# Attention tails issued one row half at a time in units 7 to 15, with a wider margin for planned idling

## The chip, the cores and the metric

The kernel is written in Bass for one Trainium2 chip and runs as one program on one of its cores. The metric is the device time of one execution in microseconds (us). A core has five engines with a queue each: TensorE (PE in the profile; its weight loads are shown as PEld), VectorE (DVE), ScalarE (ACT), GpSimd (POOL) and SyncE (SP, which here only issues DMAs). Every queue is worked off in order, and engines wait for each other by semaphores.

## The reference

Cosine-similarity attention over 8 batches, 12 heads, 448 positions and 64 dimensions, followed by a two-layer feed-forward network with the activation h cos(h) over the 3584 tokens of 768 features:

```python
q_n = q / (norm(q) + 1e-6);  k_n = k / (norm(k) + 1e-6)
attn = softmax(q_n @ k_n.T / tau)              # tau = 0.1
x = (attn @ v).transpose(0, 2, 1, 3).reshape(3584, 768)
h = x @ w_in                                   # 768 -> 2048
out = (h * cos(h)) @ w_out                     # 2048 -> 768
```

## The kernel before

**Units and groups.** A unit is half a batch, six heads; there are 16. A unit has three groups of two heads, so there are 48 groups, numbered g, with unit u = g // 3. The two heads of a group are stacked: head a lies on partitions 64a to 64a+63 of the transposed operands.

**One group's attention.** 448 key positions are three blocks of 128 and a rest of 64. `scores(g, c)` (lines 716 to 736) makes the scores of block c (c = 0 is the rest, c = 1 to 3 the full blocks) with four 64x64 products: head a uses array rows 64a to 64a+63. The rest is arranged so that all 128 rows of the result are used: the upper and the lower 64 partitions hold the rest's scores for two different halves of the queries (o = 0 and 1; the queries are seven strips of 64, each of two halves of 32 columns). ACT then takes the exponential into `PX` (full blocks) or `PH` (the rest).

`attend(g, ...)` (line 739 on) multiplies by the values and makes the sums of the exponentials. Its stages are 0 and 1 (the tails, that is the rest) and 2 (the full blocks):

- Stages 0 and 1 are `rest(e, n)`, line 761: four 64x64 products of 224 columns each. Step n multiplies the values with the half o = n, on rows 64n to 64n+63, and at the same time sums the other half on the other 64 rows, against ones. Step 1 is marked as `settled` on step 0: it waits until step 0 has ended. The scripts below write `a` for stage 0, `b` for stage 1 and `c` for stage 2.
- Stage 2 is `av` (line 768), the values against the three full blocks in four column groups of 32, and, for a group that isn't "direct", the sums: `sm` (line 776, blocks 1 and 2 side by side, 448 columns) and `sm2` (line 784, block 3, two halves of 224 columns in the four column groups).

Groups in `direct` (0 to 5, 7 to 11, 17, 23 and 47) get their reciprocals on ACT by logarithm and exponential. For the others `chain(u)` (line 885) gathers the sums of a unit with DMAs into 128 partitions (`gather`, two DMAs, line 889), adds the parts and takes the reciprocal on VectorE (lines 901 and 904), writes it to DRAM (`spread`, line 905) and reads it back broadcast (`bcast`, line 907); POOL multiplies (line 911) and so makes `xT`, the input of the first layer.

**The network.** `m1` is the first layer of one batch (96 products of 128x128 by 448 columns, line 919), with a cosine on ACT (line 948) and a product on VectorE (line 950) for each two feature blocks. The second layer works on tiles of 128 tokens: `m2_quarters` (line 1017) makes a tile with four 64x64 products at a time, 16 fours in a first half and 16 in a second, where the two row halves exchange their PSUM banks. The first four of the second half is `settled` on the last of the first. When a tile is done, VectorE copies it out of PSUM.

**Order of the work.** TensorE's order from group 19 on is written by hand in `PLAN["script"]`: `s33.0` is a score block, `f5` five fours of the second layer as filling, `m4` a first layer. All else is ordered by a planner: `arrange` computes due times from costs, and `play` runs through the work, where an engine takes the most urgent operation that is ready. It idles for one that is not yet ready if that one is due earlier by more than `PLAN["margin"]` (1.0 us) and comes within `hold` (0.6 us) or half the ready one's cost. The time before the first data is filled with warm-up products on zeros (`zt`, lines 1075 and 1076).

Of the kernel before, what the change touches and what calls it, by code (L numbers as in the profile page):

```python
# [6 lines left out]
ACT = mybir.ActivationFunctionType  # L7
ALU = mybir.AluOpType
# [10 lines left out]
    "swapped": {},  # L19
    "script": {19: """  # L20
# [8 lines left out]
        s32.1 f2 a31 f2 b31 s32.2 f5 s32.3 f7 a32 s33.0 f5 s33.1 f5 s33.2 f6 b32 c32 s33.3 f10 m4 f6  # L29
        a33 s34.0 f8 s34.1 f8 b33 c33 s34.2 f5 s34.3 f5 s35.0 f6 s35.1 f5 s35.2 f4 s35.3 f4 a34 f3 b34 s36.0 c34 c35  # L30
        s36.1 a35 f3 b35 f1 s36.2 f6 s36.3 f6 a36 s37.0 f5 s37.1 f5 s37.2 f6 b36 c36
        s37.3 f4 s38.0 f4 s38.1 f4 s38.2 f4 s38.3 f4 a37 f2 b37 s39.0 c37 c38 s39.1 a38 f3 b38 f1 s39.2 f3 s39.3 f3 m5 c39
        a39 f4 s40.0 b39 f4 s40.1 f4 s40.2 f2 s40.3 f2 s41.0 s41.1 f4 s41.2 f5 s41.3 f5 a40 f2 b40 s42.0 c40 c41
        s42.1 a41 f3 b41 f1 s42.2 f4 s42.3 f4 s43.0 f4 s43.1 f4 s43.2 f5 s43.3 f5 a42 f2 b42 s44.0 c42 c43
        s44.1 f2 a43 f2 b43 s44.2 f5 s44.3 f7 a44 s45.0 f5 s45.1 f5 s45.2 f6 b44 c44 s45.3 f10 o012 m6 f6 s46.0 a45 f12 s46.1 b45 f4 c45 s46.2 f3 s46.3 f4
# [9 lines left out]
    "margin": 1.0,  # L45
# [370 lines left out]
def bass_cosine_attention__then__act_gcu_kernel(  # L416
# [13 lines left out]
    UP = 3  # L430
# [13 lines left out]
    NT = 3  # L444
    TD, LT = PLAN["turned"], 9
# [27 lines left out]
    lnn = sbs("lnn", 2, [128, UH * NB], F32)  # L473
# [4 lines left out]
    PX = sbs("PX", 2, [128, NB * S], BF16)  # L478
    xu = sb("xu", [128, 5 * UP * S], F32)
    RB = sbs("RB", 2, [128, UP * S], F32)  # L480
    sums = sbs("sums", 2, [128, 2 * SPR], F32)
    rcp = sbs("rcp", 2, [128, SPR], F32)
# [3 lines left out]
    zt = sb("zt", [128, S], BF16)  # L486
    ones = sb("ones", [128, 128], BF16)
    iot = cosb[0].bitcast(I32).ap()[:, 0:128]
# [17 lines left out]
    PXv = [t.ap()[:, 0 : NT3 * 2 * S].rearrange("p (c a s) -> p c a s", c=NT3, a=2) for t in PX]  # L506
    PHv = [t.ap()[:, NT3 * 2 * S : NB * S].rearrange("p (a s) -> p a s", a=2) for t in PX]
    xuv = xu.ap().rearrange("p (r g s) -> p r g s", r=5, g=UP)
# [15 lines left out]
    HALF = 0.096  # L524

# [49 lines left out]
    pool(lambda e: e.memset(ones.ap().rearrange("p (x y) -> p x y", y=32)[:, 0:4:3], 0.0), (), ["zeros"], 0.12)  # L575
    sel = [gT.bitcast(F32).ap()[:, (f * RING + S) // 2 : (f * RING + S) // 2 + 128] for f in (NF - 2, NF - 1)]
# [65 lines left out]
    lnnv = [t.ap().rearrange("p (h s) -> p h s", h=UH) for t in lnn]  # L642
    rnv = [t.ap().rearrange("p (h s) -> p h s", h=UH) for t in rn]

    def rnorm(u, p0, p1, t=(0, 1)):
# [5 lines left out]
        if u in PLAN["roots"] or (u, p0) in PLAN["roots"]:  # L651
# [6 lines left out]
        act(lambda e: e.activation(lnnv[i][:, h, w], n2v[i][:, h, w], ACT.Ln, bias=cst.ap()[:, 1:2]),  # L658
            [("n2", i, p, z) for p, z in keys] + ["cst1"], [("lnn", i, p, z) for p, z in keys],
            n, "E", 1, "ln" + tag)  # L660
        act(lambda e: e.activation(rnv[i][:, h, w], lnnv[i][:, h, w], ACT.Exp, scale=-0.5),  # L661
            [("lnn", i, p, z) for p, z in keys], [("rn", i, p, z) for p, z in keys], n, "E", 0, "rn" + tag)
# [47 lines left out]
    def scores(g, c, bank=None):  # L710
# [5 lines left out]
        def full(e):  # L716
            for o in range(2):
                for a in range(2):
                    r = slice(64 * a, 64 * a + 64)
                    m = e.matmul(ph[BP * o : BP * o + BP, a, 0:S], t[r, c - 1 + (NT3 + 1) * o, 0:BP],  # L720
                                 t[r, :, BP : 2 * BP], start=True, stop=True)
            return m

        def half(e):
            for o in range(2):
                for a in range(2):
# [8 lines left out]
        act(lambda e: e.activation(PHv[j] if c == 0 else PXv[j][:, c - 1], ph[:, :, 0:n], ACT.Exp, scale=1.0 / TAU),  # L735
            keys, [("PX", j, c)], 2 * n, "E", label="exp%d.%d" % (g, c))

    opened, held, turned = {}, {}, set(PLAN["swapped"])

    def attend(g, direct, stages=(0, 1, 2)):  # L740
# [8 lines left out]
        folded, swapped = g in PLAN["folded"], g in turned  # L749

        def rest(e, n):
            for k in range(2):
                o = n ^ k
                r = slice(BP * o, BP * o + BP)
                for a in range(2):
                    w = vav[y][r, 2 * p + a, 0 if o else VS - 1, :] if k == 0 else ones.ap()[r, ws]
                    to = AVq[64 * a : 64 * a + 64, k, :, o, :]
                    if folded and k:
                        w = ones.ap()[r, 64 - 64 * o : 128 - 64 * o]
                        to = av_[64 * a : 64 * a + 64, 1, 0 : S // 2]  # L760
                    m = e.matmul(to, w, PHv[j][r, a, :],  # L761
                                 start=(n == 0 and g not in PLAN["quarters"] and not swapped), stop=(n == 1 and swapped))
            return m
# [8 lines left out]
        def sm(e):  # L772
            for n in range(2):
                for a in range(2):
                    o = 64 * a + 32 * n
                    t = e.matmul(av_[o : o + 32, 1, 0:S], ones.ap()[:, 32:64], PXv[j][:, n, a, :],
                                 start=swapped, stop=False)
            return t

        def sm2(e):  # L780
            for n in range(2):
                for a in range(2):
                    o, w = 64 * a + 32 * n, slice(S // 2 * n, S // 2 * n + S // 2)
                    t = e.matmul(av_[o : o + 32, 1, w], ones.ap()[:, 32:64], PXv[j][:, 2, a, w],  # L784
                                 start=False, stop=not swapped)
            return t
# [32 lines left out]
        for n in stages:  # L819
            if n < 2:  # L820
                o = P.op("PE", lambda e, n=n: rest(e, n), [("va", y), ("PX", j, 0), "ones", "zeros"], both_keys,
# [17 lines left out]
        if not direct:  # L839
            if 2 in stages:  # L840
                P.op("PE", sm, ["ones", ("PX", j, 1), ("PX", j, 2)], [ks], cost=MM, mode="C32", label="S%d" % g)
                P.op("PE", sm2, ["ones", ("PX", j, 3)], [ks], cost=HALF, mode="C32", label="S%d" % g)
# [3 lines left out]
            both = bass.AP(xu, (u % 3 * UP + p) * S, [[5 * UP * S, 128], [(3 + i - u % 3) * UP * S, 2], [1, S]])  # L846
# [9 lines left out]
        if folded:  # L856
            s, r = xuv[:, 3 + i, p, 0 : S // 2], RBv[i][:, p, 0 : S // 2]
# [14 lines left out]
        act(lambda e: e.activation(xuv[:, 3 + i, p, :], av_[:, 1, 0:S], ACT.Ln), [ks], [("xs", i, p)], S, "E",  # L872
            label="lnS%d" % g, bias=PLAN["bs"] if g < PB else 0.0)
        act(lambda e: e.activation(r, xuv[:, 3 + i, p, :], ACT.Exp, scale=-1.0), [("xs", i, p)], [("RB", i, p)], S, "E",  # L874
# [10 lines left out]
    def chain(u):  # L885
        i, b = u % 2, u // 2
        n = sum(UP * u + p not in PLAN["direct"] for p in range(UP))
        w = SPR // UP * n
        dma("SP", [lambda e, r=r: e.dma_start(
            sums[i].ap()[:, w * r : w * r + w],  # L890
# [462 lines left out]
```

## Time and profile before

| what | value |
|---|---|
| median of 3 runs | 421.1 us (420.59 to 423.0) |
| the profiled execution | 420.54 us, span 418.8 us |
| granted TensorE clock, mean | 0.999 |
| busy share PE, ACT, POOL, DVE | 98, 65, 58, 45% |
| second layer, fours of 64x64 (L1017) | 2816 products |
| first layer (L919) | 768 products |
| tails (L761) | 384 products |

In the profile L761 is line 761 of the kernel before. A group of instructions is shown as result <- operands, the shape of an instruction and how often it occurs (x8). Lines in the order of time begin with the start and the length in us; the end of a matrix product is modelled, and products overlap, so a slot is read from one start to the next.

### The profile page before, as it was taken

What the parts mean: (1) busy time and instruction counts of PE and PEld (TensorE: products, weight loads), DVE (VectorE), ACT (ScalarE), POOL (GpSimd) and SP (SyncE); (2) the same over time, 40 slices, a digit from 0 to 9 for tenths busy, and PEclk for the clock granted to TensorE, in tenths of its full rate; (3) what the DMA queues carried; (4) which work ended last, traced back from release to release, by engine and by line L of the source; (5) the groups of instructions that cost most, each with busy time, mean ns of one, the idle gap of its engine ahead of it and who ended that gap; (6) DMA issues with size and microseconds to landing.
All of it is one profiled execution on the core that took longest, in us unless ns stands there. A gap on an engine that the chain in (4) does not pass through costs nothing.

```text
span 418.8 us, 13571 instructions
## 1 busy us (share of the span) xinstructions
PE 409.6 (98%) x6074; PEld 236.5 (56%) x6074; DVE 189.5 (45%) x250; ACT 271.3 (65%) x363; POOL 242.7 (58%) x193
## 2 busy tenths in 40 slices
PE   7899999999999999999999999999999999999997
PEld 3354556655556555665466555665566655565565
DVE  3564744456663277124753087213862244223421
ACT  5887578983987746877498556776498745703500
POOL 4999977989761666938864782907867320020000
PEclk9999999999999999999999999999999999999999
DMA  8999999879849997579766993949966720141023
GB/s 191 251 253 226 209 223 172 213 174 198 144 104 151 207 222 185 109 168 217 168 114 127 210 242 83 147 109 212 212 123 128 161 68 3 41 121 38 2 67 85
DMA packets 80254, 63.61 MB, mean 152 GB/s; under 512 B 44996, under 2 KB 75204, under 8 KB 80196
## 3 DMA queue, kind: packets, MB, share of 16 engines
q1 hardware_dynamic: 61988, 50.06, 55.4%
q0 software_dynamic: 18048, 12.59, 20.2%
q8 instruction: 48, 0.79, 0.8%
q10 hardware_dynamic: 160, 0.10, 0.1%
q14 instruction: 10, 0.08, 0.1%
HBM read 54.98 MB, written 11.13 MB: 158 GB/s over the span
## 4 chain that ended last, share of the span: by engine, by line
PE 92%; ACT 4%; POOL 1%; DVE 1%; DMA 1%; issue 1%; SPq 0%; ACTq 0%; POOLq 0%
PE MP L1017 27%; PE SC L919 21%; PE AV L919 11%; PE SC L720 6%; PE AV L768 4%; PE MP L1046 4%; PE SC L1046 3%; PE SC L768 2%; PE AV L761 2%; PE AV L794 2%; PE MP L919 2%; ACT PX L735 2%; PE SC L728 1%; ACT cosb L948 1%; PE MP L809 1%; PE AV L1046 1%
## 5 line engine op out<-in xcount | busy, mean ns | idle before, releaser
L735 ACT ACTIVATE PX<-SC 128x896 bf16<-128x896 f32 (+1 forms) x166 | 132.8, 828 | 26.1 <-PE SC L720 18.2
L1017 PE MATMUL MP<-W,gT 64*64 64x384 bf16 x2816 | 142.3, 324 | 0.9 <-DVE qkT L707 0.6
L1017 PEld LDWEIGHTS MP<-W,gT 64*64 64x64 bf16 x2816 | 79.2, 107 | 35.7 <-PE MP L1017 3.8
L919 PE MATMUL SC<-xT,W 128*128 128x448 bf16 x468 | 94.9, 353 | 0.0
L669 POOL TENSOR_TENSOR qks<-raw,rn 128x896 bf16<-128x896 f32 (+1 forms) x48 | 79.8, 1679 | 24.6 <-ACT rn L661 24.0
L630 POOL TENSOR_TENSOR sq<-raw 128x896 bf16<-128x896 f32 x44 | 73.6, 1692 | 9.0 <-DMA raw<-in_q_dram 7.0
L948 ACT ACTIVATE cosb<-SC,cst 128x896 f32<-128x896 f32 x39 | 39.1, 1006 | 57.0 <-PE SC L919 52.6
L911 POOL TENSOR_TENSOR xT<-xu,RB 128x448 bf16<-128x448 f32 x34 | 37.8, 1136 | 60.7 <-DMA RB<-scr 60.7
L919 PEld LDWEIGHTS SC<-xT,W 128*128 128x128 bf16 x468 | 45.5, 98 | 42.8 <-ACT xu L848 0.6
L950 DVE TENSOR_TENSOR gT<-SC,cosb 128x896 bf16<-128x896 f32 x39 | 42.4, 1089 | 40.6 <-ACT cosb L948 38.3
L919 PE MATMUL AV<-xT,W 128*128 128x448 bf16 x264 | 56.7, 353 | 0.0
L984 DVE COPY osb<-MP 128x384 f32<-128x384 f32 x50 | 25.8, 553 | 66.8 <-PE MP L1017 56.1
L637 DVE TENSOR_REDUCE n<-sq 128x14 f32<-128x896 bf16 (+2 forms) x49 | 51.2, 1058 | 6.1 <-ACT sq L628 5.3
L720 PE MATMUL SC<-qkT 64*64 64x448 bf16 x504 | 45.6, 356 | 0.6 <-ACT PX L735 0.6
L919 PEld LDWEIGHTS AV<-xT,W 128*128 128x128 bf16 x264 | 25.6, 98 | 24.2 <-ACT xu L848 0.3
L948 ACT ACTIVATE cosb<-AV,cst 128x896 f32<-128x896 f32 x22 | 22.1, 1006 | 23.6 <-PE AV L919 20.7
L950 DVE TENSOR_TENSOR gT<-AV,cosb 128x896 bf16<-128x896 f32 x22 | 23.9, 1088 | 14.3 <-ACT cosb L948 14.2
L604 POOL DMA_DIRECT2D va<-in_v_dram x32 | 21.9, 692 | 7.0 <-DMA raw<-in_q_dram 4.2
L878 POOL TENSOR_TENSOR xT<-xu,RB 128x448 bf16<-128x448 f32 x8 | 9.1, 1134 | 28.5 <-ACT RB L874 28.5
L851 DVE COPY xu<-AV 128x896 f32<-128x896 f32 x13 | 14.2, 1091 | 21.5 <-PE AV L784 14.6
L552 ACT ACT_TABLE_LOAD x17 | 21.8, 1283 | 1.0 <-PEq L1335 0.7
L720 PEld LDWEIGHTS SC<-qkT 64*64 64x64 bf16 x504 | 14.4, 106 | 14.2 <-ACT PX L735 6.1
(95 smaller groups left out, 428.0 us busy)
## 6 DMA issues: line engine op xcount, KB each, us to landing
raw<-in_k_dram SPq DMA_DIRECT2D x48, 224.0 KB, 6.5
raw<-in_q_dram SPq DMA_DIRECT2D x48, 224.0 KB, 6.7
out_dram<-osb SPq DMA_DIRECT2D x54, 192.0 KB, 3.5
va<-in_v_dram POOLq DMA_DIRECT2D x32, 192.0 KB, 7.1
RB<-scr SPq DMA_DIRECT2D x18, 336.0 KB, 4.7
W<-in_moe_w_in_dram POOLq DMA_DIRECT2D x4, 768.0 KB, 15.9
W<-in_moe_w_out_dram POOLq DMA_DIRECT2D x4, 768.0 KB, 18.6
RB<-scr SPq DMA_DIRECT2D x6, 224.0 KB, 4.0
```

The source lines that it names most:

```text
L630: pool(lambda e, x=x, y=y: e.tensor_tensor(y, x, x, ALU.mult), src_, dst, 0.1 + n * 1.78e-3, label="sq%d.%d" % (u, p)).pad = LATE if u > 1 ...
L637: dve(lambda e, w=w: e.tensor_reduce(out=n2v[i][:, 2 * p : 2 * p + 2, w], in_=sqv[p][:, :, w, :], axis=mybir.AxisListType.X, op=ALU.add), ...
L669: f = lambda e, s0=s0, s1=s1: e.tensor_tensor(qksv[i][:, p, s0:s1].rearrange("p s h d -> p h s d"), rawv[i][:, h, s0:s1, :], bass.AP(rn[i] ...
L720: m = e.matmul(ph[BP * o : BP * o + BP, a, 0:S], t[r, c - 1 + (NT3 + 1) * o, 0:BP], t[r, :, BP : 2 * BP], start=True, stop=True)
L735: act(lambda e: e.activation(PHv[j] if c == 0 else PXv[j][:, c - 1], ph[:, :, 0:n], ACT.Exp, scale=1.0 / TAU), keys, [("PX", j, c)], 2 * n ...
L911: pool(lambda e, p=p: e.tensor_tensor(xTv[b % 2][:, UP * i + p, :], xuv[:, u % 3, p, :], RBv[i][:, p, :], ALU.mult), [("RB", i, p), ("xa", ...
L919: t = e.matmul(ph[:, a, 0:S], W1v[:, order[c], 128 * n : 128 * n + 128], xTv[b % 2][:, order[c], :], start=(c == 0), stop=(c == NKC - 1))
L948: act(lambda e, ph=ph, cz=cz: e.activation(cosv[cz], ph[:, :, 0:S], ACT.Sin, bias=cst.ap()[:, 0:1], scale=1.0), names(gi) + ["cst0"], [("c ...
L950: dve(lambda e, ph=ph, cz=cz, gi=gi: e.tensor_tensor(gTv[:, 2 * gi : 2 * gi + 2, S * (b % 2) : S * (b % 2) + S], ph[:, :, 0:S], cosv[cz], ...
L984: dve(lambda e: e.tensor_copy(dst, po[:, 0:n]), name, [("osb", o, hf)], n, label="osb%d" % t)
L1017: r = e.matmul(POH[b][x : x + 64, 0:HW], gTv[k, y, col + x : col + x + 64], W2v[k, y, HW * b : HW * b + HW], start=(y == 0 and h == 0), st ...
L1046: r = e.matmul(po[:, 0 : w[1] - w[0]], gTv[:, y, col : col + 128], W2v[:, y, w[0] : w[1]], start=(y == 0), stop=(y == NF - 1))
```

## The change

- `PLAN["alone"]` names units 7 to 15. In them, for groups that aren't direct, a tail step is `row(e, o)` in place of `rest`: two products only, the values against the half o, on rows 64o to 64o+63. The tail's sums move to stage 2: `sm` now opens the sums, with weights that are one in 16 columns and zero in 16, and `sm2` becomes two products of the new weights `tail` with the rest (224 columns), two with the first three quarters of block 3 (336 columns) and two with its last quarter (112 columns). The old `sm2` is now `sm1`.
- The sums of the rest's second half then lie 32 columns aside, on other partitions: the gather of these units has a third DMA, with a gap of zeros before each buffer, and the reduction adds three parts.
- `scores` and `m2_quarters` issue the products on rows 64 to 127 before those on rows 0 to 63. Before, they went by columns.
- `PH` becomes a tensor of its own with three buffers instead of a part of the two `PX` buffers.
- `margin` goes from 1.0 to 1.5.
- Some script lines move `a` and `b` of groups 32, 33, 44 and 45, and spread the filling of groups 40 and 41 otherwise.
- To make room, `lnn` goes (the logarithm is written to `rn`), `rcp` has one buffer, and `zt` lies in the third output buffer.

```diff
+    "alone": range(7, 16),
...
-        s32.1 f2 a31 f2 b31 s32.2 f5 s32.3 f7 a32 s33.0 f5 s33.1 f5 s33.2 f6 b32 c32 s33.3 f10 m4 f6
-        a33 s34.0 f8 s34.1 f8 b33 c33 s34.2 f5 s34.3 f5 s35.0 f6 s35.1 f5 s35.2 f4 s35.3 f4 a34 f3 b34 s36.0 c34 c35
+        s32.1 f2 a31 f2 b31 s32.2 f5 s32.3 f2 a32 f5 b32 s33.0 f5 s33.1 f5 s33.2 f6 c32 s33.3 f10 m4 a33 f6
+        b33 s34.0 f8 s34.1 f8 c33 s34.2 f5 s34.3 f5 s35.0 f6 s35.1 f5 s35.2 f4 s35.3 f4 a34 f3 b34 s36.0 c34 c35
...
-        a39 f4 s40.0 b39 f4 s40.1 f4 s40.2 f2 s40.3 f2 s41.0 s41.1 f4 s41.2 f5 s41.3 f5 a40 f2 b40 s42.0 c40 c41
+        a39 f4 s40.0 b39 f4 s40.1 f4 s40.2 f4 s40.3 f2 s41.0 f2 s41.1 f3 s41.2 f3 s41.3 f4 a40 f2 b40 s42.0 c40 c41
...
-        s44.1 f2 a43 f2 b43 s44.2 f5 s44.3 f7 a44 s45.0 f5 s45.1 f5 s45.2 f6 b44 c44 s45.3 f10 o012 m6 f6 s46.0 a45 f12 s46.1 b45 f4 c45 s46.2 f3 s46.3 f4
+        s44.1 f2 a43 f2 b43 s44.2 f5 s44.3 f4 a44 f3 b44 s45.0 f5 s45.1 f5 s45.2 f6 c44 s45.3 f10 o012 m6 a45 f6 b45 s46.0 f12 s46.1 f4 c45 s46.2 f3 s46.3 f4
...
-    "margin": 1.0,
+    "margin": 1.5,
...
-            for o in range(2):
-                for a in range(2):
+            for a in (1, 0):
+                for o in range(2):
                     r = slice(64 * a, 64 * a + 64)
...
+        def row(e, o):
+            r = slice(BP * o, BP * o + BP)
+            for a in range(2):
+                m = e.matmul(AVq[64 * a : 64 * a + 64, 0, :, o, :], vav[y][r, 2 * p + a, 0 if o else VS - 1, :], PHv[g % 3][r, a, :],
+                             start=(o == 0 and not swapped), stop=(o == 1 and swapped))
             return m
...
         def sm(e):
+            w = ones.ap()[:, 80:112] if alone else ones.ap()[:, 32:64]
             for n in range(2):
                 for a in range(2):
                     o = 64 * a + 32 * n
-                    t = e.matmul(av_[o : o + 32, 1, 0:S], ones.ap()[:, 32:64], PXv[j][:, n, a, :],
-                                 start=swapped, stop=False)
+                    t = e.matmul(av_[o : o + 32, 1, 0:S], w, PXv[j][:, n, a, :], start=alone or swapped, stop=False)
             return t
...
+        def sm2(e):
+            for a in range(2):
+                e.matmul(AVq[64 * a + 32 : 64 * a + 64, 1, :, 0, :], tail.ap(), PHv[g % 3][:, a, :], start=False, stop=False)
+            for a in range(2):
+                e.matmul(av_[64 * a : 64 * a + 32, 1, 0:SH], ones.ap()[:, 80:112], PXv[j][:, 2, a, 0:SH], start=False, stop=True)
+            for a in range(2):
+                t = e.matmul(av_[64 * a + 32 : 64 * a + 64, 1, SH:S], ones.ap()[:, 80:112], PXv[j][:, 2, a, SH:S],
+                             start=False, stop=True)
             return t
...
+            if n < 2 and alone:
+                o = P.op("PE", lambda e, n=n: row(e, n), [("va", y), ("PH", g % 3)], [ka], cost=HALF - 0.006 if n else 0.008,
+                         mode="Q", label="R%d" % g)
...
+        w, m = SPR // UP * n, 3 if u in PLAN["alone"] else 2
...
+            sums[i].ap()[:, w * r : w * r + w], bass.AP(xu, x, [[64 * XW, 2], [w, 64], [1, w]]))
+            for r, x in enumerate((XS[i], 32 * XW + XS[i], 48 * XW + XS[i] - HQ)[:m])], ["gap"] + [("xs", i, p) for p in range(n)], [("sums", i)], "sums%d" % i, 0.7,
...
-                for x in range(0, 128, 64):
-                    for z in range(2):
+                for z in (1, 0):
+                    for x in range(0, 128, 64):
                         k, b = slice(64 * z, 64 * z + 64), z ^ h
```

## The prediction

> **What bounds the kernel now.** I read the busy shares first, then the busy time by stretch, then TensorE's own order of time. The first two say that TensorE is the bound almost everywhere:
>
> ```profile
> span 418.8 us, 13571 instructions
> ...
> PE 409.6 (98%) x6074; PEld 236.5 (56%) x6074; DVE 189.5 (45%) x250; ACT 271.3 (65%) x363; POOL 242.7 (58%) x193
> ...
> 0.00:34.00 34.00, 29.37 (x350) 14.40 (x351) 19.16 (x34) 26.15 (x50) 28.48 (x31) 1.00 1.08 235
> ...
> 155.00:376.00 221.00, 220.77 (x3584) 129.78 (x3582) 95.72 (x126) 146.17 (x183) 121.02 (x91) 1.00 0.70 142
> ```
>
> The units that the change rewrites, 7 to 15, lie in the last stretch. PE is busy there for 220.77 of 221 us; from 150 to 376 us its weight loads wait 2.2 us for ACT and 0.4 us for VectorE, mostly ahead of their turn, its products 0.2 us. So in that stretch a slot that PE gains or loses moves the end by its own length, and work on the other engines costs nothing until it makes PE wait. The starts in the order of time give the price of a slot:
>
> ```profile
> 185.31 0.26 PE L761 MATMUL SC<-PX,va 64*64 64x224 bf16 x1
> ...
> 185.32 0.26 PE L761 MATMUL SC<-PX,ones 64*64 64x224 bf16 x1
> 185.40 0.50 PE L1017 MATMUL MP<-W,gT 64*64 64x384 bf16 x8
> ...
> 185.73 0.26 PE L761 MATMUL SC<-PX,ones 64*64 64x224 bf16 x1
> ...
> 185.82 0.27 PE L728 MATMUL SC<-qkT 64*64 64x224 bf16 x4
> ...
> 326.82 0.33 PE L1017 MATMUL MP<-W,gT 64*64 64x384 bf16 x4
> ...
> 327.08 0.27 PE L728 MATMUL SC<-qkT 64*64 64x224 bf16 x4
> 327.23 0.68 PE L1017 MATMUL MP<-W,gT 64*64 64x384 bf16 x12
> ```
>
> Four 64x64 products start within 10 ns and hold the array together: from start to start, four of 224 columns take 96 ns, of 384 columns 163 ns, of 448 columns 189 ns (medians of all starts in the trace). The first lines are a tail's first step (L761, 185.31), then come two fours of the second layer (x8), then its second step (185.73).
>
> That distance of 0.41 us is also where a wait is about to bind. The second step waits for the first one's end. Its weight load starts 326 to 330 ns after the first step's last start whenever little lies between, and where nothing else holds it the product starts 3 ns later. Where a second-layer tile changes over from its first half to its second (327.23), the same kind of wait on the last 384-column four gives 395 ns, so that 163 + 96 + 96 = 355 ns of work between the two is not enough, and PE loses 40 ns, and 24 ns more because the weights could not be loaded ahead (the next four then takes 187 instead of 163).
>
> **The change, part by part.** Units 7 to 15 have 27 groups; 23 and 47 are direct, so 25 groups get the new tails.
>
> *Tail rows.* Before: two steps of four, 2 x 96 = 192 ns. After: the first step is two products on rows 0 to 63 only, the second two on rows 64 to 127, and the work between is issued with rows 64 to 127 first. If the upper half runs one 96 ns slot ahead from the first step until the second, both cost one slot and some 6 ns of starts: 102 ns, a gain of 90. The bounds are 0 and 90. I take 90, because the trace has such a stagger:
>
> ```profile
> 113.95 0.76 PE L1017 MATMUL MP<-W,gT 64*64 64x384 bf16 x12
> 114.46 0.44 PE L720 MATMUL SC<-qkT 64*64 64x448 bf16 x4
> 114.65 0.26 PE L761 MATMUL AV<-PX,ones 64*64 64x224 bf16 x1
> 114.71 0.26 PE L761 MATMUL AV<-PX,va 64*64 64x224 bf16 x1
> 114.74 0.26 PE L761 MATMUL AV<-PX,ones 64*64 64x224 bf16 x1
> ```
>
> The four of L761 start spread over 90 ns; the spread arose at 113.95 and went through three fours of L1017 and one of L720 at their usual 163 and 189 ns.
>
> *Sums.* The 224-column sums of the third block (four products, 96 ns) become two of 224, two of 336 and two of 112 columns, in four 32-column groups, each of which streams 336 columns: 140 ns and two starts of 2.5, 145 ns. No row has this shape; one slot of 96 ns below and two of them, 192, above bound it, so 0 to +96 per group; I take +49, by the columns.
>
> *Sum per group*: -90 + 49 = -41 ns, where nothing else binds. Three kinds of groups differ.
> - Nine groups (25, 26, 28, 30, 31, 37, 40, 42, 43) have two second-layer fours between the steps. The second step is now free at 6 + 326 = 332 ns, and its load may start at 328: no idle time, but no load ahead either, 24 ns (row 66.57 to 66.69 us of the trace: a step with no load ahead takes 120 ns, not 96). -17 each.
> - Groups 32, 33, 44 and 45 now put the second step just before a change of halves. The last second-layer four then ends one slot later in its lower half, so the 395 ns count from 96 ns later. Before, the first step lay in that gap for nothing. +96 + 6 - 96 + 49 = +55 each.
> - Groups 36 (a change of halves right after its first step) and 22 (PE stands 0.2 us after its first step, at 168.5) hide the first step already: +49 each.
>
> The other ten: -0.41 us. Together -0.41 - 0.15 + 0.22 + 0.10 = **-0.24 us**.
>
> *The line of groups 40 and 41.* Two scores with no filling between them cost a stall before:
>
> ```profile
> 308.49 0.49 PE L1017 MATMUL MP<-W,gT 64*64 64x384 bf16 x8
> 308.82 0.27 PE L728 MATMUL AV<-qkT 64*64 64x224 bf16 x4
> 309.27 0.38 PE L720 MATMUL SC<-qkT 64*64 64x448 bf16 x4 [0.19 <-ACT PX L735]
> 309.49 0.33 PE L1017 MATMUL MP<-W,gT 64*64 64x384 bf16 x4
> ```
>
> From the last four (308.65) to the next is 0.82 us, against 163 + 96 + 190 = 449 ns of work: 375 ns lost. Two fours now lie between the two scores; the change of halves falls behind s40.3 and costs the usual 67. **-0.31 us**. The total of fours is the same (22). What is late next are s41.2 and s41.3, with three fours each, 0.68 us per score against 0.92 us of an exponential (L735): if ACT cannot lead, up to 2 x 0.2 us come back.
>
> *Order of four products* (L1017, L720, L728), rows 64 to 127 first: L794 and L761 are issued row by row already and take 189 and 96 ns. Nothing. Were it not so, it is 704 + 192 fours, 0.9 us for each ns.
>
> *Third gather* in nine units: 0.58 us of SP and little landing. In unit 7 SP stands still from 175.7 to 177.5, and the spread goes out only at 178.77, behind a transpose, while the reciprocal ended at 177.57; so nothing. Later units finish their last product for the first layer 1.5 us or more before PE needs it (unit 11: 288.4 against 289.9). The reduction over 63 instead of 42 numbers adds some 10 ns on VectorE (182 ns for 28, 190 for 42). Past SP go the transposes; the shortest time from a transpose's issue to its scores is 5.0 us (group 43) against 3.6 us to land. Without this cover it is 9 x 0.6 = 5 us at most.
>
> *Three buffers for the half block, one `rcp`, no `lnn`*: the waits that they move end microseconds before anyone needs them (spread of one unit and sum of the next lie 7.6 us or more apart). Nothing.
>
> *Start*: five small memsets on VectorE, 60 ns each, two with a wait, ahead of the zeros for the warm-up products: 0.3 to 0.4 us.
>
> ```profile
> 1.59 0.24 DVE L1075 MEMSET zt<- 128x224 uint32 x1
> ...
> 1.90 6.22 PE L1076 MATMUL MP<-zt 128*128 128x448 bf16 x24 [1.90 <-DVE zt L1075]
> ...
> 8.46 0.40 PE L693 MATMUL MP<-ident,qks 128*128 128x128 bf16 x4 [0.35 <-POOL qks L669]
> ```
>
> The 24 products end at 8.11, PE then waits 0.35 us for the first data: cover for just this. Nothing.
>
> *Margin 1.5.* Working the plan's rule through for the kernel before gives 48 chosen idles, and five had an urgency between 1.0 and 1.5 us: one on POOL at unit 3, one on VectorE at unit 13, three on ACT, where a copy (`xu`, 0.91 us) or a norm would go ahead of an exponential of groups 21, 23 and 28. ACT idles 1.19 us at 140.7 before its exponential, so the copy fits. From -0.3 to +3 x 0.6 us; I take 0.
>
> Sum: -0.24 - 0.31 = **-0.55 us on the profiled execution's 420.54: 420.0 us**. That execution is 0.56 us below the median shown, 421.1 (420.59 to 423.0).
>
> **The rule that speaks against it.** The Trainium skill, "TensorE: Matmul & The Clock Gate", Part 3, says that a weight load overlaps with products in flight only when its row group differs. By it the pairs on one row group would each show their load, 107 ns by the rows of L761: 25 x 0.107 = 2.7 us, 422.7 in all. The trace disagrees: at 185.31 the four loads of L1017 start while L761 is in flight in all four quarters, and fours stay at 163 ns. What is left of it is in the first rival's chance.
>
> **The rivals.**
> - *The halves do not run beside each other*, or every four pays a late load while they are apart. Then each step keeps its slot: 25 x 90 = 2.25 us back, 422.2; or about 108 fours between the steps at 24 ns, 2.6 us, 422.6. The stagger at 114 us speaks against it. It decides for slower from 24 ns per four on. 0.12.
> - *Slower: the new plan makes ACT or POOL late for PE in the first 60 us*, where PE already loses 8 us in pieces of up to 0.81 us (55.7). An exponential put behind one ACT operation costs 0.9 us, three of them 2.7: 422.7. For it: that stretch has no spare ACT (26.15 of 34 us busy) and the plan is made anew. Against: few choices flip. 0.14.
> - *Faster: the same new plan takes such pieces away*, three of 0.6 to 0.8: 418.0. 0.12.
> - *Warm-up*: PE starts on 373 ns slots and goes to 190 at 4.86. If zeros that come 0.4 us later move this out by the whole warm-up, all 24 take 373: they end at 11.2, 2.7 us late, 422.7. 0.05.
> - *My forecast*, 420.0, or 418.8 to 421.4 by the bounds of the sums' slot: 0.57.
>
> **How the numbers follow.** Runs of this kernel differ by about 0.5%, or 2.1 us, so against the 420.54 that the sum goes by, 418.4 to 422.6 is no change. The forecast lies within, and of the first rival nearly all: 0.68. Faster (0.13) is the third rival; slower (0.19) is the second and the warm-up. The range reaches from the faster rival to the slower ones, 418.2 to 422.8.
>
> **What would show it.** Right: between the steps fours at 163 ns with two starts about 96 ns behind the other two; second steps of two-four groups about 330 ns after the first; a last sums step of 145 ns; changes of halves of about 490 ns at groups 32, 33, 44 and 45; no 0.4 us hole at 309. Wrong: fours above 163 ns, the first transposes after 8.6 us, or new waits of PE for ACT before 60 us.

## The result and the profile after

The changed kernel takes 420.18 us (median of 21 runs, 419.79 to 421.36) against 421.1 us for the kernel before (21 runs, 420.56 to 423.0): a ratio of 0.9975, with a 95% interval of 0.9968 to 0.9982. That is 0.25% less, within the 0.5% that the prediction counts as no change, and 0.2 us from the 420.0 us predicted. The profiled execution of the changed kernel took 420.87 us, so it lies above its own median, as that of the kernel before (420.54 us) lies below its own.

The span and the busy shares on the page of the changed kernel:

```profile
span 419.1 us, 13485 instructions
...
PE 410.7 (98%) x6024; PEld 241.2 (58%) x6024; DVE 189.9 (45%) x255; ACT 271.3 (65%) x363; POOL 242.8 (58%) x193
```

and its busy time in the first 34 us and in the part with units 7 to 15 (columns: window, its length, then busy us and instructions of PE, PEld, DVE, ACT and POOL, the clock, the DMA share and GB/s):

```profile
0.00:34.00 34.00, 30.12 (x349) 14.76 (x350) 19.30 (x39) 26.03 (x50) 28.40 (x31) 1.00 1.08 231
...
155.00:376.00 221.00, 220.96 (x3536) 133.58 (x3535) 96.79 (x127) 146.07 (x184) 121.41 (x91) 1.00 0.73 145
```

TensorE is still busy in all of the second window. The new tail in the order of time, at group 25 (L778 is `row`, L1052 the second layer, L738 the scores of the rest, L785 the values of the full blocks, L809, L807 and L811 the last sums step):

```profile
185.94 0.26 PE L778 MATMUL SC<-PH,va 64*64 64x224 bf16 x2
186.03 0.49 PE L1052 MATMUL MP<-W,gT 64*64 64x384 bf16 x6
186.26 0.28 PE L778 MATMUL SC<-PH,va 64*64 64x224 bf16 x2
186.37 0.28 PE L738 MATMUL SC<-qkT 64*64 64x224 bf16 x4
...
187.35 0.31 PE L809 MATMUL SC<-PX,ones 128*32 128x336 bf16 x1
...
187.45 0.22 PE L811 MATMUL SC<-PX,ones 128*32 128x112 bf16 x2
187.49 0.36 PE L785 MATMUL AV<-PX,va 128*32 128x448 bf16 x4
```

The second step starts 318 ns after the last start of the first, and the next scores 111 ns after the second. Sums that took one slot of 96 ns now go from 187.35 to 187.49. The hole of the kernel before at 309 us, between the scores of groups 40 and 41, is gone:

```profile
309.22 0.36 PE L730 MATMUL SC<-qkT 64*64 64x448 bf16 x4
309.47 0.52 PE L1052 MATMUL MP<-W,gT 64*64 64x384 bf16 x8
309.82 0.27 PE L738 MATMUL AV<-qkT 64*64 64x224 bf16 x4
309.92 0.50 PE L1052 MATMUL MP<-W,gT 64*64 64x384 bf16 x8
310.24 0.36 PE L730 MATMUL SC<-qkT 64*64 64x448 bf16 x4
```

**Where the time went.** I matched the starts of the same scores and products in both traces. Two parts have to be kept apart.

- *From the first scores of group 21 (138.63 us before) to the last product* the changed kernel is 0.53 us shorter. This difference repeated to 0.01 us in the two kernels that I profiled twice. I call it "the stretch" below.
- *Ahead of it* the profiled execution of the changed kernel is 0.84 us longer, in pieces of 0.14 to 0.44 us that appear in one execution and not in the next: ahead of group 21 a second execution of the same kernel is 0.05 us ahead of the kernel before, and a second execution of the kernel before is 0.25 us behind the first. No wait for another engine is shown at them.

The largest of these pieces begin inside one step of PE, as in the second execution of the kernel before, where one product of four scores starts and three come 0.45 us later:

```profile
113.74 0.26 PE L728 MATMUL SC<-qkT 64*64 64x224 bf16 x1
114.19 0.29 PE L728 MATMUL SC<-qkT 64*64 64x224 bf16 x3 [0.19 <-issue]
```

The kept traces point at a cause. In those of the two kernels and of all experiments but the last (row tails from unit 5 on), each piece of 0.16 us and more behind group 1 begins behind one of four products of PE's program (the 854th, 1108th, 1487th or 2884th), the same in every execution that stops there. Ahead of each of them lies a 16 KB transfer that the trace's DMA records list under "instruction". PE stopped in all nine cases where it reached such a product less than 1.3 us after the end of that transfer, and in none of the 32 where it took more than 1.4 us. In the execution shown the transfer began at 111.66 us, in the first one at 110.34. So PE seems to wait for its own code, which lands at another time in each execution; no experiment tests this.

So single executions can't tell 0.5 us by their total, but the stretch can, as long as no such piece falls into it (one does, see the whole tails below).

| part, in ns of the stretch | predicted | measured |
|---|---|---|
| ten groups, plain gain (21, 24, 27, 29, 34, 35, 38, 39, 41, 46) | -410 | -424 |
| nine groups with two fours between the steps | -153 | +84 |
| groups 32, 33, 44, 45 | +220 | +215 |
| groups 22 and 36 | +98 | +52 |
| line of groups 40 and 41 | -310 | -296 |
| margin | 0 | -167 |
| sum | -555 | -536 |

The line's -296 comes from the experiment with it alone, and the margin's -167 from the one place that it moves; the rest is read from the changed kernel's trace against the one before, group by group. Group 40 is what is left when the line's gain is taken as in the kernel before.

### The profile page after: what moved, and what is told of

Its sections match the earlier page's. It is cut to its first block, busy times and chain, and to the rows that moved or that the text cites. A ratio compares the mean times of both kernels' runs of the same rounds, so it can differ in the third digit from the quotient of the medians.

```text
span 419.1 us, 13485 instructions
## 1 busy us (share of the span) xinstructions
PE 410.7 (98%) x6024; PEld 241.2 (58%) x6024; DVE 189.9 (45%) x255; ACT 271.3 (65%) x363; POOL 242.8 (58%) x193
## 4 chain that ended last, share of the span: by engine, by line
PE 92%; ACT 3%; POOL 1%; DVE 1%; DMA 1%; issue 0%; SPq 0%; ACTq 0%; POOLq 0%
PE MP L1052 27%; PE SC L954 21%; PE AV L954 11%; PE SC L730 6%; PE AV L785 4%; PE MP L1081 4%; PE SC L1081 3%; PE SC L785 2%; PE AV L821 2%; PE MP L954 2%; ACT PX L745 1%; PE AV L771 1%; PE SC L738 1%; PE AV L730 1%; PE MP L836 1%; PE AV L1081 1%
## 5 line engine op out<-in xcount | busy, mean ns | idle before, releaser
L1052 PE MATMUL MP<-W,gT 64*64 64x384 bf16 x2816 | 143.6, 324 | 1.0 <-DVE qkT L717 0.4
L745 ACT ACTIVATE PX<-SC 128x896 bf16<-128x896 f32 x125 | 112.2, 918 | 17.3 <-PE SC L730 14.6
L1052 PEld LDWEIGHTS MP<-W,gT 64*64 64x64 bf16 x2816 | 83.7, 107 | 34.4 <-PE MP L1052 4.8
L679 POOL TENSOR_TENSOR qks<-raw,rn 128x896 bf16<-128x896 f32 (+1 forms) x48 | 79.8, 1680 | 19.6 <-ACT rn L671 19.2
L1019 DVE COPY osb<-MP 128x384 f32<-128x384 f32 x50 | 25.8, 553 | 79.0 <-PE MP L1052 62.8
L985 DVE TENSOR_TENSOR gT<-SC,cosb 128x896 bf16<-128x896 f32 x39 | 42.4, 1090 | 38.0 <-ACT cosb L983 37.8
L985 DVE TENSOR_TENSOR gT<-AV,cosb 128x896 bf16<-128x896 f32 x22 | 23.9, 1088 | 14.1 <-ACT cosb L983 14.0
L745 ACT ACTIVATE PH<-SC 128x448 bf16<-128x448 f32 x39 | 21.3, 547 | 5.8 <-PE SC L738 5.4
L887 DVE COPY xu<-AV 128x896 f32<-128x896 f32 x12 | 13.0, 1087 | 19.5 <-PE AV L801 7.7
```

What stands on the lines that cost most here:

```text
L679: f = lambda e, s0=s0, s1=s1: e.tensor_tensor(qksv[i][:, p, s0:s1].rearrange("p s h d -> p h s d"), rawv[i][:, h, s0:s1, :], bass.AP(rn[i] ...
L745: act(lambda e: e.activation(PHv[g % 3] if c == 0 else PXv[j][:, c - 1], ph[:, :, 0:n], ACT.Exp, scale=1.0 / TAU), keys, [("PX", j, c) if ...
L985: dve(lambda e, ph=ph, cz=cz, gi=gi: e.tensor_tensor(gTv[:, 2 * gi : 2 * gi + 2, S * (b % 2) : S * (b % 2) + S], ph[:, :, 0:S], cosv[cz], ...
L1019: dve(lambda e: e.tensor_copy(dst, po[:, 0:n]), name, [("osb", o, hf)], n, label="osb%d" % t)
L1052: r = e.matmul(POH[b][x : x + 64, 0:HW], gTv[k, y, col + x : col + x + 64], W2v[k, y, HW * b : HW * b + HW], start=(y == 0 and h == 0), st ...
```

## The experiments

Medians are set against runs of the kernel before in the same set: 421.15 us in the first set, 420.73 in the second, 421.02 in the third.

**The two kernels again.** No edit.

> The changed kernel once more. In its first profile the stretch from the first scores of group 21 to the last product is 0.53 us shorter than before, and the stretch ahead of it 0.84 us longer, though the median of its runs is 0.92 us shorter. If the TensorE slots are the cause, the stretch behind group 21 is 0.5 to 0.55 us shorter again, to 0.1 us. If what lies ahead of group 21 is chance from run to run, it differs from the first profile by 0.3 us or more; if it belongs to the new plan, it is 0.84 us longer again, with the same holes at 72 and 83 us.

Measured: 420.19 us, ratio 0.9976 (0.9965 to 0.9986); the stretch -0.53 us. The losses at 72 and 83 us that the first profile of the changed kernel shows aren't there.

> The kernel before against itself. Behind group 21 it should repeat its profile to 0.1 us. The changed kernel gains 0.9 us by its runs, but only 0.53 us of it lies behind group 21, so some 0.4 us must lie ahead, where the two profiles differ by +0.84 and -0.05 us. If the first profile of before caught a fast execution, this one takes up to 0.6 us more ahead of group 21, by holes that the first one has not. If it repeats that stretch to 0.2 us, the 0.4 us are not to be seen in profiles.

Measured: 420.82 us, ratio 1.0004 (0.9991 to 1.0017); the stretch -0.01 us, and ahead of it +0.25 us, from the one piece at 113.74 us that is shown above. What follows: these pieces belong to the execution, not to the change.

**The order of the four products.**

```diff
-            for a in (1, 0):
-                for o in range(2):
+            for o in range(2):
+                for a in range(2):
...
-                for z in (1, 0):
-                    for x in range(0, 128, 64):
+                for x in range(0, 128, 64):
+                    for z in range(2):
```

> The changed kernel with the four products of scores and second layer issued by columns again. By the theory that a tail step costs little only because the row halves run apart, each first step now holds the array for a slot: ten plain groups lose 90 ns, nine with two fours between the steps 62, four at a change of halves 25, which is 1.56 us, 1.2 to 1.8: about 421.7 us, or 1.0 us over before in the stretch behind group 21. By the rival that half the products cost half the time in any order, the time stays at 420.2 and the stretch 0.5 us under before.

Measured: 420.13 us, ratio 0.9977 (0.9966 to 0.9987); the stretch -0.49 us. My theory, that rows 64 to 127 must be issued first for the tails to run beside other work, fell. The order of time at group 25 with columns first:

```profile
185.29 0.49 PE L1052 MATMUL MP<-W,gT 64*64 64x384 bf16 x8
185.62 0.26 PE L778 MATMUL SC<-PH,va 64*64 64x224 bf16 x1
185.62 0.32 PE L1052 MATMUL MP<-W,gT 64*64 64x384 bf16 x1
185.62 0.26 PE L778 MATMUL SC<-PH,va 64*64 64x224 bf16 x1
185.63 0.58 PE L1052 MATMUL MP<-W,gT 64*64 64x384 bf16 x7
185.94 0.28 PE L778 MATMUL SC<-PH,va 64*64 64x224 bf16 x2
```

The tail's two products hold rows 0 to 63 from 185.616 and .623. Two products of the next four start at 185.619 and .626, the other two at 185.712 and .719. The trace doesn't name the rows of a product, but with rows 0 to 63 held the first two can only be those on rows 64 to 127, and these were issued second and fourth. So a product started when its own quarter was free, ahead of one issued before it. That every queue is worked off in order, as the opening has it, is too strong for such starts. The Trainium skill, "TensorE: Matmul & The Clock Gate", Part 3, says that products start and end strictly in the order of issue; for the starts this trace disagrees, and it decides; the ends in it are modelled and show nothing. All that the new order brings is at the changes of halves with a row step just ahead: 463 to 478 ns instead of 480 to 491, 0.04 us in all.

**The tails.** Whole tails with all else as changed, and row tails with the order of the work as before.

```diff
-    "alone": range(7, 16),
+    "alone": (),
```

> The changed kernel with no unit in alone: whole tail steps, two gathers, old sums, with the new order of products, script, margin and buffers. By the slots: against before the line of groups 40 and 41 gives 0.28 us, and groups 32, 33, 44 and 45 lose 0.38 us (96 ns each), because their first steps no longer lie in a gap that is there anyhow: 0.1 us over before in the stretch behind group 21, 0.6 us over the changed kernel. If margin, buffers or order gave the gain, it stays at 420.2 us.

Measured: 420.53 us, ratio 0.9986 (0.9974 to 0.9997); the stretch +0.08 us, which is near the 0.1 us expected only because of a piece of 0.25 us at 187.6 us, of the kind described above. (The kernel before with margin 1.5 loses 0.05 us at the same product.) Without that piece it is -0.17, so the row tails bring some 0.36 us with the new lines. The new lines cost the whole tails some 0.29 us, about 95 ns each at groups 32, 33 and 44 and next to nothing at group 45. But the cause isn't the one expected: the changes of halves take what they took before (395 to 402 ns from the last start). The second step has gone from between two output tiles, and the first four of the next tile comes 302 ns after the scores instead of 214, because it waits for VectorE's copy of the finished tile (L1019):

```profile
235.12 0.11 PEld L730 LDWEIGHTS AV<-qkT 64*64 64x64 bf16 x4 [0.28 <-issue]
235.42 0.14 PEld L1052 LDWEIGHTS MP<-W,gT 64*64 64x64 bf16 x8 [0.19 <-DVE osb L1019]
```

Now the script.

```diff
-        s32.1 f2 a31 f2 b31 s32.2 f5 s32.3 f2 a32 f5 b32 s33.0 f5 s33.1 f5 s33.2 f6 c32 s33.3 f10 m4 a33 f6
+        s32.1 f2 a31 f2 b31 s32.2 f5 s32.3 f7 a32 s33.0 f5 s33.1 f5 s33.2 f6 b32 c32 s33.3 f10 m4 f6
... the lines of groups 34, 40 and 44 to 46 alike
```

> The changed kernel with the script of before. By the slots: 0.28 us lost at groups 40 and 41, and 25 ns each at groups 32, 33, 44 and 45 (a gap of about 405 ns and a second step of 96, against 6 and 470): 0.4 us over the changed kernel, 420.6 us, and 0.15 us under before in the stretch behind group 21. By my own prediction of 491 ns for those changes of halves the four groups would gain 6 ns each instead: 0.25 us over the changed kernel.

Measured: 420.19 us, ratio 0.9972 (0.9961 to 0.9982); the stretch -0.39 us. The line of groups 40 and 41 is missed (from the first scores of group 40 to those of 42 the gain is 0.03 instead of 0.28 us), but groups 32, 33, 44 and 45 are some 0.1 us cheaper than with the new lines. The moves didn't pay. Less the margin's part, the row tails bring some 0.2 us here. The first scores of group 42 start 108 ns behind group 40's second step here, against 214 ns in the changed kernel: the wait behind group 40 comes with its new line.

**The margin.** One number, on either kernel: 1.5 in the kernel before, 1.0 in the changed one.

> The kernel before with the margin at 1.5 alone. By my prediction a margin costs nothing and gives nothing: 421.1 us, ratio 1.000. By the rival that the new plan gives what lies ahead of group 21 it takes 0.4 to 0.6 us less, 420.6 us.

Measured, in the kernel before: 420.82 us, ratio 0.9999 (0.9989 to 1.001); the stretch -0.13 us.

> The changed kernel with the margin back at 1.0. By my prediction 420.2 us, as the changed one; by the rival that the margin gives the rest of the gain 420.6 us. Behind group 21 both expect 0.5 us under before.

Measured, the changed kernel with 1.0: 420.27 us, ratio 0.9981 (0.9969 to 0.9992); the stretch -0.32 instead of -0.53 us. Runs can't resolve this, the traces can. There is one place, at group 24. ACT and the scores there, in the kernel before:

```profile
171.51 0.92 ACT L735 ACTIVATE PX<-SC 128x896 bf16<-128x896 f32 x1 [0.79 <-PE SC L720]
172.33 0.91 ACT L848 ACTIVATE xu<-AV 128x896 f32<-128x896 f32 x1
173.12 2.33 ACT L735 ACTIVATE PX<-SC 128x896 bf16<-128x896 f32 x3
...
174.10 0.11 PEld L720 LDWEIGHTS SC<-qkT 64*64 64x64 bf16 x4 [0.35 <-ACT PX L735]
```

and with margin 1.5 and no other change:

```profile
171.24 0.92 ACT L848 ACTIVATE xu<-AV 128x896 f32<-128x896 f32 x1 [0.47 <-PE AV L784]
172.05 3.27 ACT L735 ACTIVATE PX<-SC 128x896 bf16<-128x896 f32 x4
...
174.00 0.36 PE L720 MATMUL SC<-qkT 64*64 64x448 bf16 x4
```

With 1.0 ACT idles for an exponential, and the copy that was ready lands between two exponentials, at 172.33. With 1.5 the copy goes first, at 171.24, the four exponentials follow each other, and the scores at 174.10 no longer wait for ACT. They and the step behind them come 0.17 us earlier, all of it PE's time. In the changed kernel 0.21 us hang on it, as the wait at 1.0 also takes the 0.04 us that the row tail of group 21 saves. (In the kernel before 0.05 us are lost again at 187.6 us, the piece named above, which makes -0.13.)

**The line of groups 40 and 41 alone**, the script line that begins with `a39`, as the change has it, in the kernel before.

> The kernel before with the new line of groups 40 and 41 alone. Theory: the 375 ns hole at 308.8 goes, and the first scores of group 42 start 0.26 to 0.31 us earlier, with everything ahead of them and behind them in step with the kernel before; runs 0.3 us under before. Rival (group 41's last scores wait for ACT with only three second-layer fours between them): 0.1 us or less is left of it.

Measured: 421.06 us, ratio 1.0001 (0.9989 to 1.0013); in the trace both kernels stay in step to within 0.01 us up to group 40, the line is 0.30 us shorter, and both are in step again behind it. The runs can't show these 0.3 us: they spread from 420.17 to 422.73, and the interval reaches from -0.5 to +0.5 us.

**Three fours instead of two** between the steps of the nine groups, in the changed kernel.

```diff
-        ... s26.3 f3 a25 f2 b25 s27.0 c25 c26
+        ... s26.3 f2 a25 f3 b25 s27.0 c25 c26
... and eight more
```

> The changed kernel with three instead of two fours between the tail steps of groups 25, 26, 28, 30, 31, 37, 40, 42 and 43, each taken from the filling just ahead or behind. By the wait of some 317 ns on the first step, weights can then be loaded ahead: up to 24 ns each, 0.2 us less behind group 21 than the changed kernel, 0.73 us under before. By the rival that what follows waits for ACT anyhow (the first scores of groups 30 and 42 start 217 ns behind the step before them instead of 111) it is 0.1 us or nothing.

Measured: 420.12 us, ratio 0.9986 (0.9976 to 0.9995); the stretch -0.68 us, 0.15 less than the change. It isn't nine equal shares, though: four groups (25, 30, 37, 42) gain 36 ns each, and five keep nothing. Behind groups 28 and 40 the next scores start no earlier; behind 26, 31 and 43 they start 6 to 7 ns earlier and lose it again soon after. What holds them at group 26, in the changed kernel (ACT's line is the exponential, PEld's the load for the scores behind it):

```profile
188.94 0.92 ACT L745 ACTIVATE PX<-SC 128x896 bf16<-128x896 f32 x1 [1.69 <-PE SC L730]
...
189.30 0.37 PE L730 MATMUL SC<-qkT 64*64 64x448 bf16 x4
...
189.90 0.11 PEld L730 LDWEIGHTS SC<-qkT 64*64 64x64 bf16 x4 [0.28 <-ACT PX L745]
189.91 0.38 PE L730 MATMUL SC<-qkT 64*64 64x448 bf16 x4
```

The exponential that frees the bank ends at 189.85, and the scores start 53 ns behind it. Up to the scores ahead, at 189.30, the row tail had saved 89 ns; 88 of them go in this wait. In the kernel before it was there already, just covered:

```profile
189.24 0.11 PEld L720 LDWEIGHTS SC<-qkT 64*64 64x64 bf16 x4 [0.20 <-ACT PX L735]
```

This is a round of scores, exponential and scores again: the exponential at 188.94 had itself waited for the scores at 188.50, and from these to those at 189.91 it takes 1.41 us in both kernels. A slot saved inside such a round brings nothing. Behind group 28 ACT has no pause at all (L778 is the tail's second step, L738 the next scores):

```profile
215.05 0.95 ACT L745 ACTIVATE PX<-SC 128x896 bf16<-128x896 f32 x1
215.85 0.96 ACT L745 ACTIVATE PX<-AV 128x896 bf16<-128x896 f32 x1
216.65 0.97 ACT L745 ACTIVATE PX<-SC 128x896 bf16<-128x896 f32 x1
...
216.73 0.28 PE L778 MATMUL SC<-PH,va 64*64 64x224 bf16 x2
216.95 0.29 PE L738 MATMUL AV<-qkT 64*64 64x224 bf16 x4
```

The scores at 216.95 start 144 ns after the end of the exponential from 215.85. In six more traces with this wait it is 144 ns too, and behind group 40 it is 144 or 145.

**The rest of the change**, without row tails, with the order and the margin of before.

```diff
-    "alone": range(7, 16),
+    "alone": (),
...
-    "margin": 1.5,
+    "margin": 1.0,
... and all script lines as before
```

> The change without its three parts of the stretch: tails as before in all units, order of the groups as before, margin 1.0. What is left are the order of four products, the three buffers, the small memsets at the start and the moved warm-up zeros. Theory: nothing from the first scores of group 21 on (within 0.05 us in the trace), and runs within 0.2 us of before; the difference of 0.4 us by which the changed kernel's runs on the first chip stood below what its trace explains is chance of the runs of before. Rival: that 0.4 us belongs to these parts, and the runs come out 0.4 us under before.

Measured: 420.76 us, ratio 0.9996 (0.9987 to 1.0004); the trace is in step with the kernel before all the way, +0.03 us at group 21 and +0.03 at the last product. The order of products, the buffers and the memsets cost nothing and bring nothing in this trace.

**The own lines, and three fours.** The lines of groups 32 to 34 and 44 to 46 as before, that of 40 and 41 as changed, three fours in the nine groups.

> The change with the lines of groups 32 to 34 and of 44 to 46 as before (the first step back in the gap at the change of halves, and a whole step of the tail between two output tiles) and with three second-layer fours instead of two between the steps of the nine groups. Theory: from the first scores of group 21 to the last product 0.15 us less than the change for the three fours, and 0.15 to 0.2 us less for the lines, as the rows there cost a longer change of halves (about 75 ns) and make the first four of the next tile wait for VectorE's copy (about 46 ns): 0.8 to 0.9 us under before in that stretch, runs at about 0.85 under. Rival (the line moves paid after all): 0.5 to 0.7 under.

Measured: 419.85 us (419.58 to 420.5), ratio 0.9974 (0.9964 to 0.9983); the stretch -0.83 us. It is the fastest in this study by the stretch; against the changed kernel itself it was not run in the same set, and the two ratios overlap. The changes of halves at groups 32, 33, 44 and 45 are back at 405 ns. The other half of the reason is VectorE's copy of a finished output tile, L1019 (L984 before). In the kernel before, around the tile that ends ahead of 234 us:

```profile
233.07 0.98 PE L1017 MATMUL MP<-W,gT 64*64 64x384 bf16 x20
...
234.17 1.02 DVE L984 COPY osb<-MP 128x384 f32<-128x384 f32 x2 [4.55 <-PE MP L1017]
...
235.04 0.38 PE L720 MATMUL AV<-qkT 64*64 64x448 bf16 x4
235.25 1.16 PE L1017 MATMUL MP<-W,gT 64*64 64x384 bf16 x24
```

and in the changed kernel:

```profile
233.60 1.14 PE L1052 MATMUL MP<-W,gT 64*64 64x384 bf16 x24
...
234.87 1.02 DVE L1019 COPY osb<-MP 128x384 f32<-128x384 f32 x2 [4.63 <-PE MP L1052]
...
235.69 0.38 PE L730 MATMUL AV<-qkT 64*64 64x448 bf16 x4
235.94 0.52 PE L1052 MATMUL MP<-W,gT 64*64 64x384 bf16 x8
```

The new line takes the tail's second step out from between the two tiles. The copy, which lasts 1.02 us and sits between the last four of one tile and the first of the next, now ends last: the scores at 235.69 and the next four at 235.94 lie 250 ns apart, against 214 before, and the four behind takes 7 ns longer. That is 43 to 46 ns a time at three of the four tiles. At the fourth, at group 46, the kernel before waits for the copy already (302 ns); there the change wins 48 ns.

**Row tails from unit 5 on**, added to that version.

```diff
-    "alone": range(7, 16),
+    "alone": range(5, 16),
```

> As the version with its own lines, and with the row tails from unit 5 on instead of 7. Theory: groups 15 to 20 gain up to 41 ns each, 0.25 us at most, where PE waits for nothing else; ACT holds PE more often there, as at groups 26 and 28, so 0 to 0.25 us under the version with its own lines. Rival: units 5 and 6 wait for ACT, whose exponentials follow each other, and nothing is gained or the third gather makes them late: the same or slower.

Measured: 424.28 us (421.43 to 428.2, 6 runs), ratio 1.0062 (1.0037 to 1.0086): slower. The profiled execution, 428.2 us, is the slowest of the six, so the size of its loss is not typical. The other five, 421.43 to 425.19 us, left no trace: that they lose time at the same place is likely, not shown. SP's queue there, in the order of time:

```profile
146.69 1.56 SPq L696 DMA_TRANSPOSE qkT<-qks  x1
148.35 8.94 SPq L925 DMA_DIRECT2D sums<-xu  x3
157.34 2.91 SPq L601 DMA_DIRECT2D raw<-in_k_dram  x1
```

and the one wait of PE's products between 140 and 173 us (what waits, for what, us in total, times, the longest):

```profile
PE SC L954 <- DVE gT L985: 3.4, 1, 3.4
```

The three issues of unit 6's gather hold SP for 8.94 us instead of the 1.64 us of two in the version without, and the last one lands at 161.45. VectorE, whose queue holds the reduction of these sums, comes late with the product `gT` (L985), which must free a bank of PSUM before the first layer can go on; PE loses 6.5 us between the first layer's start at 145.9 and the scores of group 22: some 3.6 us stand still, and behind that 17 products take 373 ns each instead of 189, with a granted clock of 0.59 from 165 to 170 us. That the third DMA alone makes the queue so slow there wasn't tried by itself.

**What the runs say beside the stretch.** In the first set all four kernels lie 0.4 to 0.7 us further below the kernel before than their stretch explains, and so does the changed kernel itself (-0.92 by medians, -0.53 in the stretch). In the second and third set the two differ by -0.3 to +0.4 us, with both signs. A cause in the kernel would have to show in the run of the rest of the change alone, and that trace shows none; but its interval, -0.55 to +0.17 us, doesn't exclude 0.4 us. This part stays open.

## Why the prediction was right, point by point

The total of the stretch is right, -0.53 for -0.55 us, and four of its six terms are, each to within 0.05 us. Two are not, and it is chance that they nearly cancel: +237 ns at the nine two-four groups against -167 ns of the margin. That the median, 420.18 us, lies so near 420.0 is chance too: the sum went by an execution 0.56 us below the median of the kernel before, and by the medians the change brings 0.92 us, of which 0.39 us are not explained.

- *Tail rows: a gain of 90.* Right. Where nothing else binds, the next scores start 89 to 97 ns earlier. Between the steps the products on the two row halves start 102 ns apart at the groups with two fours (73 to 113 ns at most others), and the fours keep 163 ns. What carries it is that a quarter starts when it is free; the order of issue, which I had put first, isn't needed.
- *Sums: +49, by the columns.* Right: 45 to 54 ns in every group.
- *Ten groups at -41.* Right: -20 to -48, together -424.
- *Nine two-four groups at -17 each.* Wrong, and this is the step that failed: "a gain of 90" was taken there on the condition "where nothing else binds", and I didn't look for what binds. The second step does come as soon as its wait allows, 318 ns after the last start of the first and 322 after its first (I had 332). But at groups 26, 28 and 40 the next scores then wait for an exponential, and these three come out at +52, +91 and +88. At 216 us, behind group 28, ACT starts one every 0.80 us without a pause; PE can't get further ahead there. I had named such a limit for groups 40 and 41 alone, under *what is late next*. The 2.2 us that I read as PE's waits for ACT are those for exponentials; with the copies `xu` they are 2.8.
- *Groups 32, 33, 44 and 45 at +55.* Right in sum, by errors that cancel. From the first start of the last four, the change of halves takes 463 to 478 ns instead of 405, so 58 to 73 ns more, where I had 96. What I left out is VectorE's copy of the tile, 43 to 46 ns lost at three of them and 48 ns won at the fourth. Groups 32, 33 and 44 cost 74 to 80 ns, and group 45 gained 19.
- *Groups 36 and 22 at +49.* Group 36 costs 48. Group 22 costs 4: PE waits for its next scores in any case.
- *Line of groups 40 and 41: -0.31.* Right, -0.30.
- *Margin 1.5: 0.* Wrong. I had bounded it by -0.3 and +1.8 us and put it at zero because "the copy fits" at group 21. At the exponential of group 23, which I had also named, it didn't fit; the next scores, of group 24, come 0.17 us earlier.
- *Start.* The warm-up products began 0.4 us later, as predicted. But the mark that I had set, the first transposes after 8.6 us, came true (9.22) without the cost: the first scores are 0.47 us late, those of group 1 0.08. As a mark it says little, as the second execution of the kernel before has 8.66 us. This first fall-back is covered by what PE waits for next, the product on POOL (L679).
- *Third gather: 0.58 us of SP.* The cost to the end was nothing, as predicted, but not the size: issues of this gather hold SP for 4.1 to 4.6 us in units 8, 10 and 12 of the changed kernel, while the first layer runs. The cover was there; in unit 6 it isn't.
- *The rivals.* None came about. The halves run beside each other. In its second execution the changed kernel stays within 0.15 us of the one before from group 1 to group 21. The warm-up did move out by 2.2 us, as that rival had it, but what follows covered it.

## What to carry to other kernels

A slot saved on the engine that is always busy counts only up to the next place where another engine is paced: go through the sites one by one, and for each ask which wait ends just before it. Where a step is moved, look at what its time had been covering, here a copy of 1.02 us and the gap of a self-wait. And when a change is worth a thousandth, compare the starts of the same instructions in two traces by sections; medians of 6 to 35 runs couldn't place 0.3 us.

## What the runs showed of the hardware that I had not expected

- A 64x64 product started ahead of one issued before it, when its quarter was free and the other's wasn't (3 ns against 96 ns behind the step), as far as start times and the order of issue tell.
- The warm-up products change from 373 to 190 ns at 5.0 to 6.6 us when they start at 1.90 us (four executions), and at 5.4 to 8.2 us when they start at 2.30 us (eight). The first transposes come at 8.60 us after a change at 5.8, at 9.22 us after one at 7.3. The start of the changed kernel in the order of time:

```profile
2.30 7.08 PE L1111 MATMUL MP<-osb 128*128 128x448 bf16 x24 [2.30 <-DVE osb L1110]
9.22 0.39 PE L703 MATMUL MP<-ident,qks 128*128 128x128 bf16 x4
```

and that of the version with three fours:

```profile
2.30 6.30 PE L1111 MATMUL MP<-osb 128*128 128x448 bf16 x24 [2.30 <-DVE osb L1110]
8.60 0.40 PE L703 MATMUL MP<-ident,qks 128*128 128x128 bf16 x4
```

The Trainium skill, "TensorE: Matmul & The Clock Gate", Part 1, says that the clock's window runs on its own and doesn't begin with the kernel, so that the change comes at another place from run to run; these executions agree, but they differ by 1.6 and 2.7 us, more than the 500 ns either way that the section gives.
- Small DMAs of the same kind cost SP 0.58 us at the median, and up to 2.7 us in the kernel before and 4.6 us in the changed one, at places where the first layer runs.
- Sections of the trace repeat to 0.01 us, apart from pieces of up to 0.44 us that follow a late transfer of instructions.
